# A feed-forward stage beside the attention: its last two experts take two PSUM banks in turn instead of three

## The chip, the cores and the metric

The kernel runs on one core of one Trainium2 chip. The time is device time of one execution in microseconds; the figure for a kernel is the median of its runs. TensorE (PE) does the matrix products, ScalarE (ACT) and VectorE (DVE) read their results out of PSUM, GpSimd (POOL) works on SBUF alone, and SyncE (SP) issues the DMAs.

## The reference

Three stages follow each other on 2304 tokens of width 512. All of it is in fp32.

- Attention over 4 batches, 8 heads, 576 positions of 64: scores, of each row only the 32 largest are kept, softmax over these, product with v.
- A first layer: `h = x @ w_in` (512 to 2048), `g = h * cos(h)`, `x2 = g @ w_out` (2048 to 512).
- A mixture of 8 experts: gate weights P come from `x2 @ w_gate` by eight rounds of row and column normalisation; each expert is `relu(x2 @ w1[e]) @ w2[e]` (512 to 1024 to 512), and the output is the sum over the experts of P[:, e] times its result, for all tokens.

## The kernel before

**Arithmetic.** An fp32 product is made of three matmuls of reduced precision: each operand is split into a high and a low part, and high by high, low by high and high by low are added up in one PSUM bank (`mm3`, lines 372 to 374). A weight block of 128x512 is loaded to a buffer `raw`; ACT copies its high part to `whi` (L345), POOL subtracts for the low part `wlo` (L347; in the layers after the attention DVE does that).

**Stages.** The first three tiles of 128 tokens (LEAD = 3) are taken through attention and the first layer early, then the rest of the attention runs batch by batch. It is DVE work above all: to find the 32nd largest score of a row takes four MAX8 and three MATCH_REPLACE8 over 576 columns per tile (L459, L464, L465), then one pass that masks and sums (L466). PE does little for it: the scores (L447, L448), the transposes (L475) and the product with v (L501, L503).

**Fill.** So that PE has work beside the attention, the experts of finished tokens are run beside it. `fill(e, t0, k, h_ring)` (line 762) does expert e for k tiles from t0: for each of 8 blocks f of the hidden width, 12 matmuls make `h` in a bank that it takes from `h_ring` (4 chunks of the model width, three matmuls each), `gates` reads it out twice (L758 on ACT: relu and high part `gh`; L759 on DVE: low part `gl`), and one block later 12 matmuls by w2 add to the four banks y0 to y3. After the eighth block y0 to y3 are copied to `st` (L788) and stored to `y_d`. Eight experts are filled beside batches 0 and 1 with tiles 0 to 2, a first layer of four tiles runs beside batch 1, and eight experts beside batches 2 and 3 with tiles 3 to 6. This last loop, the second block of fills, is the one that the change is in.

**Banks.** PSUM has eight: y0 to y3, `h`, `t` (transposes and the product with v), `s` (scores) and `g`. `two` is a cycle over `g` and `h`, `three` one over `g`, `s` and `h` (line 1004). Each call takes the next bank of the cycle. The scores of every attention tile go to `s`, and ACT reads them out (L457).

**Order.** Nothing is issued as it is written. Every operation is added to a plan with a cost, what it reads and writes and a priority by engine and kind of work (line 28: on PE attention 2 goes ahead of 3 for everything here called mlp, fills included; on DVE mlp 0 goes ahead of attention 2). An operation depends on the earlier ones *in program order* that wrote what it reads, and on those that read or wrote what it writes. `issue` (line 150) then plays the engines forward, takes the ready operation of the lowest priority number each time, and that makes each engine's fixed order. On the chip an engine goes through its order one by one and waits at each for its semaphores. In program order the attention of batches 2 and 3 stands wholly ahead of the eight fills.

**After.** `moe1` runs the first layer for the remaining tokens in three parts over the cycle `three` (lines 1027 to 1029), with a sixth weight buffer `ch`/`cl` (line 1024) in the pool `ph2`, which opens when the last user of the pools `att` and `ph1` is done: attention and the fills' input `x2fh` are among those. Its first five blocks by w_in and the sixth weight, of w_out, take the six buffers in turn. Then comes the mixture for the rest of the tokens, to the end.

```
    two, three = Cycle([ps_g, ps_h]), Cycle([ps_g, ps_s, ps_h])
    ...
    for b in range(2, B):
        attention(b)
    for e in range(NE):
        fill(e, LEAD, 4, two if e < 6 else three)
```

Of the kernel before, what the change touches and what calls it, by code (L numbers as in the profile page):

```python
# [217 lines left out]
def act_ns(n, psum=False, ap=False):  # L218
    return (51.0 if psum else 93.0) + n / 1.2 + (93.0 if ap else 0.0)
# [10 lines left out]
def fused_kernel(tc, kq, vv, w_in, w_out, w_gate, w1, w2, out, B=4):  # L230
# [14 lines left out]
    LEAD, FILL, MIXED = 3, 7, 8  # L245
# [16 lines left out]
    def put(eng, cost, emit, reads=(), writes=(), func=None, nbytes=0):  # L262
        return add(eng, cost, emit, reads, writes, PRIORITY[eng][CLASSES.index(work)], func, nbytes)

    def dma(dst, src, nbytes, reads=(), writes=(), slow=False):
        put("SP", 650.0 if slow else 475.0, lambda: nc.sync.dma_start(dst(), src()), reads, writes, nbytes=nbytes)
# [85 lines left out]
    def split_weight(src, dst=None):  # L352
        raw = raw_r()
        dma(lambda: raw.ap, lambda: src, 1 << 18, writes=[raw])
        hi, lo = dst or (whi_r(), wlo_r())
        split_cols((hi, lambda: hi.ap), (lo, lambda: lo.ap), (raw, lambda: raw.ap), eng=eng_w)
        return hi, lo
# [12 lines left out]
    def mm3(o, ob, ah, al, bh, bl, n, start, stop, bufs):  # L370
        def emit():
            T_.matmul(o(), ah(), bh(), start=start, stop=False)  # L372
            T_.matmul(o(), ah(), bl(), start=False, stop=False)  # L373
            T_.matmul(o(), al(), bh(), start=False, stop=stop)  # L374

        put("PE", 3 * mm_ns(n), emit, bufs, [ob])
# [378 lines left out]
    def gates(v, vb, n, g_r, psum):  # L755

        gh, gl = g_r()
        put("ACT", act_ns(n, psum=psum), lambda: A_.activation(gh.ap[:, :n], v(), AF.Relu), [vb], [gh])  # L758
        put("DVE", dve_ns(n), lambda: V.scalar_tensor_tensor(gl.ap[:, :n], v(), 0.0, gh.ap[:, :n].bitcast(F32), op0=ALU.max, op1=ALU.subtract), [vb, gh], [gl])  # L759
        return gh, gl  # L760

    def fill(e, t0, k, h_ring):

        n, pend = 128 * k, []

        def second(f, gh, gl):
            oh, ol = split_weight(w2[e, f])
            for t in range(k):
                c = slice(t * 128, t * 128 + 128)
                mm3(lambda t=t: ps_y[t].ap, ps_y[t], lambda c=c: gh.ap[:, c], lambda c=c: gl.ap[:, c], lambda: oh.ap, lambda: ol.ap,  # L770
                    512, f == 0, f == NF2 - 1, [oh, ol, gh, gl])

        for f in range(NF2):
            wh, wl = split_weight(w1[e, f])
            pb = h_ring()
            for c in range(4):
                s = slice(c * 128, c * 128 + 128)
                iv = (c * 512, c * 512 + 512)
                mm3(lambda pb=pb: pb.ap[:, :n], pb, lambda s=s, wh=wh: wh.ap[:, s], lambda s=s, wl=wl: wl.ap[:, s],
                    lambda c=c: x2fh.ap[:, c, :n], lambda c=c: x2fl.ap[:, c, :n], n, c == 0, c == 3, [wh, wl, (x2fh, *iv), (x2fl, *iv)])  # L780
            pend.append((f, *gates(lambda pb=pb: pb.ap[:, :n], pb, n, lambda: (gh_r(), gl_r()), True)))
            if len(pend) > 1:
                second(*pend.pop(0))
        second(*pend.pop(0))
        for t in range(k):
            st = st_r()
            i = e * FILL + t0 + t
            put("ACT", act_ns(512, psum=True), lambda t=t, st=st: A_.activation(st.ap, ps_y[t].ap, AF.Copy), [ps_y[t]], [st])  # L788
            dma(lambda t=t: y_d.ap[e, t0 + t], lambda st=st: st.ap, 1 << 18, [st], [(y_d, i, i + 1)])
# [214 lines left out]
    two, three = Cycle([ps_g, ps_h]), Cycle([ps_g, ps_s, ps_h])  # L1004
# [7 lines left out]
    for b in range(2, B):  # L1012
        attention(b)
    for e in range(NE):
        fill(e, LEAD, 4, two if e < 6 else three)


    eng_w = eng_r = eng_g = "DVE"
# [75 lines left out]
```

## Time and profile before

| | us |
|---|---|
| median of 3 runs | 2526.36 (2522.58 to 2527.22) |
| the profiled execution | 2523.42 |
| its span, first to last instruction | 2521.6 |
| PE busy | 2389.5 (95%) |
| DVE busy | 1981.5 (79%) |
| ACT busy | 1272.9 (50%) |
| POOL busy | 1265.6 (50%) |

The profile is of one execution. A view by windows gives each engine's busy time in a stretch and the clock that TensorE was granted there, 1.00 being 2.4 GHz and 0.50 1.2 GHz. In a timeline each line has the start in us, the duration, engine, line and operation, output <- inputs, and in brackets the idle time before it with what ended it. Matmuls overlap: one lasts some 0.39 us, and the next starts 0.23 us after it, so starts are compared, not durations.

### The profile page before, as it was taken

Reading aid. Unit: us, or ns where it says so; the run is one execution under the profiler, and the core shown is the slowest. Engines: PE = TensorE matmul, PEld = TensorE weight load, DVE = VectorE, ACT = ScalarE, POOL = GpSimd, SP = SyncE. Lnnn points to the kernel's source line nnn. Section 1 sums busy time; section 2 is a strip of 40 time slices with the busy share of each in tenths; the row PEclk is TensorE's granted clock in tenths of the full one; section 3 lists DMA queues with packets and bytes.
Section 4 is the critical chain, followed back from the end, with each engine's and each line's share of the span. In section 5 each row is a group of like instructions: output and inputs, shape, how many; then the busy total and the mean of one; then the engine's idle time right before and its main releaser. Section 6 shows DMA issues by size and latency. Waiting matters only on the chain.

```text
span 2521.6 us, 33547 instructions
## 1 busy us (share of the span) xinstructions
PE 2389.5 (95%) x11089; PEld 1919.8 (76%) x11089; DVE 1981.5 (79%) x3651; ACT 1272.9 (50%) x2438; POOL 1265.6 (50%) x1328
## 2 busy tenths in 40 slices
PE   6888999999889999997799999999999999999999
PEld 3444688888667877776588788788888888888887
DVE  8997599999989999999927778776666665666655
ACT  6785576666578656565346767422222222232221
POOL 6886587777676656565340113533333434444330
PEclk9779999999899999998799999999999999999999
DMA  8765654444322433332043333112222221111101
GB/s 265 228 211 185 201 155 150 137 139 131 99 91 78 120 116 117 109 117 77 26 132 114 106 108 115 48 55 79 71 72 84 84 72 34 34 34 46 38 21 46
DMA packets 159501, 261.37 MB, mean 104 GB/s; under 512 B 15008, under 2 KB 60656, under 8 KB 159328
## 3 DMA queue, kind: packets, MB, share of 16 engines
q1 hardware_dynamic: 159328, 259.24, 33.9%
q8 instruction: 87, 1.43, 0.2%
q14 instruction: 86, 0.70, 0.1%
HBM read 227.31 MB, written 31.87 MB: 103 GB/s over the span
## 4 chain that ended last, share of the span: by engine, by line
PE 56%; DVE 22%; POOL 4%; issue 3%; ACT 3%; DMA 1%; POOLq 0%; ACTq 0%; DVEq 0%
PE y L372 9%; PE y L373 9%; PE y L374 9%; DVE wk L464 6%; DVE m L465 5%; DVE ex L466 3%; PE g L374 2%; PE g L373 2%; PE g L372 2%; DVE atl L494 2%; DVE m L459 2%; POOL wlo L347 1%; PE y L383 1%; PE y L384 1%; PE y L387 1%
## 5 line engine op out<-in xcount | busy, mean ns | idle before, releaser
L347 POOL TENSOR_TENSOR wlo<-raw,whi 128x512 fp32r<-128x512 f32 x336 | 452.7, 1351 | 203.0 <-ACT whi L345 131.9
L465 DVE MAX8 m<-wk 128x8 f32<-128x576 f32 x432 | 318.0, 748 | 1.8
L953 DVE SCALAR_TENSOR_TENSOR acc<-y,P,acc 128x512 f32<-128x512 f32 x308 | 229.2, 748 | 103.4 <-PE y L374 103.0
L345 ACT ACTIVATE whi<-raw 128x512 fp32r<-128x512 f32 x416 | 258.9, 626 | 97.3 <-PE y L374 34.0
L464 DVE MATCH_REPLACE8 wk<-m,wk 128x576 f32<-128x576 f32 x288 | 213.6, 742 | 1.2
L475 PE MATMUL t<-ident,ex 128*128 128x128 f32 (+1 forms) x720 | 143.3, 301 | 55.8 <-DVE atl L494 20.6
L475 PEld LDWEIGHTS t<-ident,ex 128*128 128x128 f32 (+1 forms) x720 | 89.5, 145 | 122.3 <-DVE atl L494 32.4
L372 PE MATMUL y<-whi,gh 128*128 128x512 f32 x448 | 181.6, 405 | 0.0
L372 PE MATMUL y<-gh,xh 128*128 128x512 f32 x450 | 176.0, 391 | 1.0 <-DVE acc L949 1.0
L374 PE MATMUL y<-whi,gl 128*128 128x512 f32 x448 | 176.5, 394 | 0.0
L373 PE MATMUL y<-wlo,gh 128*128 128x512 f32 x448 | 175.9, 393 | 0.0
L373 PE MATMUL y<-gl,xh 128*128 128x512 f32 x450 | 175.5, 390 | 0.0
L374 PE MATMUL y<-gh,xl 128*128 128x512 f32 x450 | 175.4, 390 | 0.0
L457 ACT ACTIVATE sc<-s 128x288 f32<-128x288 f32 x288 | 117.0, 406 | 97.4 <-DVE ex L466 55.6
L466 DVE SCALAR_TENSOR_TENSOR ex<-sc,m,ex 128x576 f32<-128x576 f32 x144 | 149.7, 1039 | 3.6 <-ACT ex L461 1.8
L493 ACT ACTIVATE ath<-t 64x128 fp32r<-64x128 f32 (+3 forms) x272 | 104.5, 396 | 58.9 <-PE t L475 52.2
L470 POOL TENSOR_SCALAR ex<-ex,m 128x576 f32<-128x576 f32 x144 | 111.4, 774 | 38.1 <-DVE m L469 36.0
L461 ACT ACTIVATE ex<-sc,m 128x576 f32<-128x576 f32 x144 | 111.2, 772 | 32.1 <-POOL m L460 31.0
L459 DVE MAX8 m<-sc 128x8 f32<-128x576 f32 x144 | 106.9, 743 | 8.7 <-ACT sc L457 8.6
L464 DVE MATCH_REPLACE8 wk<-m,sc 128x576 f32<-128x576 f32 x144 | 106.7, 741 | 0.0
L468 POOL TENSOR_SCALAR m<-m 128x1 f32<-128x1 f32 x144 | 29.2, 202 | 146.5 <-DVE ex L466 141.3
L372 PEld LDWEIGHTS y<-gh,xh 128*128 128x128 f32 x450 | 84.5, 188 | 19.6 <-DVE acc L949 1.8
(384 smaller groups left out, 7150.5 us busy)
## 6 DMA issues: line engine op xcount, KB each, us to landing
raw<-in_w_dram SPq DMA_DIRECT2D x384, 256.0 KB, 2.6
kq<-in_kq_dram SPq DMA_DIRECT2D x32, 576.0 KB, 4.1
raw<-win_d SPq DMA_DIRECT2D x64, 256.0 KB, 3.0
raw<-wout_d SPq DMA_DIRECT2D x64, 256.0 KB, 2.7
y_d<-st SPq DMA_DIRECT2D x56, 256.0 KB, 3.0
raw<-y_d SPq DMA_DIRECT2D x56, 256.0 KB, 2.6
wp<-win_d SPq DMA_DIRECT2D x24, 512.0 KB, 5.0
wp<-wout_d SPq DMA_DIRECT2D x24, 512.0 KB, 4.4
```

The costliest lines, as they stand in the source:

```text
L345: put("ACT", act_ns(n), lambda: A_.activation(hv(), rv(), AF.Copy), [rb], [hb])
L347: put(e, c, lambda: f.tensor_tensor(lv(), rv(), hv().bitcast(F32), op=ALU.subtract), [rb, hb], [lb])
L372: T_.matmul(o(), ah(), bh(), start=start, stop=False)
L373: T_.matmul(o(), ah(), bl(), start=False, stop=False)
L374: T_.matmul(o(), al(), bh(), start=False, stop=stop)
L457: put("ACT", act_ns(288, psum=True), lambda c=c: A_.activation(sc.ap[:, c], o(), AF.Copy), [ps_s], [(sc, c.start, c.stop)])
L459: put("DVE", 669, lambda: V.max(mc(0, 8), sc.ap), [sc], [(m, 0, 8)])
L464: put("DVE", 669, lambda r=r, src=src: V.match_replace(wk.ap, mc(8 * r, 8), src.ap, LOWEST), [src, (m, 8 * r, 8 * r + 8)], [wk])
L465: put("DVE", 669, lambda r=r: V.max(mc(8 * r + 8, 8), wk.ap), [wk], [(m, 8 * r + 8, 8 * r + 16)])
L466: put("DVE", 729, lambda: V.scalar_tensor_tensor(ex.ap, sc.ap, mc(31), ex.ap, op0=ALU.is_ge, op1=ALU.mult, accum_out=mc(33)), [sc, ex, (m, ...
L475: T_.transpose(pt()[:p, c - c0, :], ex.ap[:, c * 128 : c * 128 + p], ident.ap)
L953: put("DVE", 663, lambda y=y, av=av, pcol=pcol: V.scalar_tensor_tensor(av(), y.ap, pcol(), av(), op0=ALU.mult, op1=ALU.add), [y, P, a], [a])
```

## The change

All eight fills of the second block take their `h` bank from `two`; experts 6 and 7 no longer take `s` in their turn. The two cycles keep a running position: `two` is called 16 times more, `three` 16 times less, so that the first-layer parts behind it begin at `g` where they began at `s`. No operation is added or left out.

```diff
     for b in range(2, B):
         attention(b)
     for e in range(NE):
-        fill(e, LEAD, 4, two if e < 6 else three)
+        fill(e, LEAD, 4, two)
```

## Rows read from the trace of the kernel before

**Rows 1.** The page's part 2: busy tenths in 40 slices of 63 us.

```profile
PE   6888999999889999997799999999999999999999
DVE  8997599999989999999927778776666665666655
```

**Rows 2.** Windows: length, busy us by engine (PE, PEld, DVE, ACT, POOL), clock, DMA.

```profile
820.00:1155.00 335.00, 329.76 (x1658) 267.10 (x1657) 329.54 (x716) 203.05 (x436) 203.67 (x259) 1.00 0.38 114
1155.00:1174.50 19.50, 19.46 (x105) 15.71 (x103) 19.23 (x43) 14.33 (x31) 12.37 (x16) 1.00 0.40 117
1610.00:2521.60 911.60, 905.26 (x4121) 762.68 (x4120) 589.37 (x877) 244.90 (x427) 339.94 (x294) 1.00 0.18 55
```

**Rows 3.** Timeline of PE around the dip, and one line of ACT.

```profile
1174.13 0.40 PE L374 MATMUL g<-x2fh,wlo 128*128 128x512 f32 x1
1175.27 0.30 PE L475 MATMUL t<-ident,ex 128*64 128x128 f32 x1 [0.75 <-DVE atl L494]
...
1232.24 0.41 ACT L457 ACTIVATE sc<-s 128x288 f32<-128x288 f32 x1 [0.92 <-PE s L448]
...
1232.70 0.79 PE L372 MATMUL s<-x2fh,whi 128*128 128x512 f32 x1
...
1321.94 0.39 PE L374 MATMUL y<-whi,gl 128*128 128x512 f32 x1
1322.17 0.39 PE L372 MATMUL s<-xh,whi 128*128 128x512 f32 x1
```

**Rows 4.** Windows between those seams, same columns.

```profile
1174.13:1232.70 58.57, 30.09 (x108) 20.74 (x106) 57.86 (x134) 23.07 (x51) 14.94 (x32) 0.60 0.07 18
1232.70:1271.50 38.80, 36.42 (x170) 28.91 (x170) 28.93 (x66) 15.16 (x32) 16.25 (x19) 0.94 0.21 59
1271.50:1322.17 50.67, 50.67 (x221) 41.34 (x220) 8.82 (x13) 22.10 (x38) 23.07 (x18) 1.00 0.47 139
```

**Rows 5.** Waits of PE, 1174.13 to 1232.7: total us, times, longest.

```profile
PE s L447 <- ACT sc L457: 10.5, 13, 2.6
PE t L475 <- DVE atl L494: 9.9, 7, 2.1
```

**Rows 6.** Timeline of the DMAs that SP issued there.

```profile
1208.06 31.16 SPq L266 DMA_DIRECT2D x_d<-x  x4
```

**Rows 7.** DVE by line, 1000 to 1100: busy us, mean ns, idle.

```profile
L465 DVE MAX8 m<-wk 128x8 f32<-128x576 f32 x38 | 28.0, 747 | 0.1
...
L466 DVE SCALAR_TENSOR_TENSOR ex<-sc,m,ex 128x576 f32<-128x576 f32 x13 | 14.9, 1144 | 0.1
...
L759 DVE SCALAR_TENSOR_TENSOR gl<-g,gh 128x512 fp32r<-128x512 f32 x7 | 4.7, 674 | 0.0
L759 DVE SCALAR_TENSOR_TENSOR gl<-h,gh 128x512 fp32r<-128x512 f32 x6 | 4.0, 672 | 0.0
```

**Rows 8.** The same by line, 1174.5 to 1232.7.

```profile
L465 DVE MAX8 m<-wk 128x8 f32<-128x576 f32 x25 | 18.3, 747 | 0.0
...
L466 DVE SCALAR_TENSOR_TENSOR ex<-sc,m,ex 128x576 f32<-128x576 f32 x9 | 7.5, 829 | 0.1
```

**Rows 9.** Window 1174.13 to 1271, line L759 (gl) alone: DVE busy, times.

```profile
1174.13:1271.00 96.87, 3.40 (x5) 0.74 0.13 34
```

**Rows 10.** Timeline of DVE: end of the attention, first use of cl.

```profile
1256.67 0.82 DVE L466 SCALAR_TENSOR_TENSOR ex<-sc,m,ex 128x576 f32<-128x576 f32 x1
...
1270.99 0.48 DVE L509 TENSOR_TENSOR x<-t,avt 64x320 f32<-64x320 f32 x1 [2.22 <-ACT avt L508]
...
1322.27 0.69 DVE L347 TENSOR_TENSOR cl<-raw,ch 128x512 fp32r<-128x512 f32 x1 [1.21 <-ACT ch L345]
```

**Rows 11.** Timeline of PE and DVE: two h banks read out.

```profile
1283.25 0.39 PE L374 MATMUL g<-x2fh,wlo 128*128 128x512 f32 x1
...
1284.31 0.69 DVE L759 SCALAR_TENSOR_TENSOR gl<-g,gh 128x512 fp32r<-128x512 f32 x1 [2.12 <-ACT gh L758]
1289.85 0.69 DVE L759 SCALAR_TENSOR_TENSOR gl<-s,gh 128x512 fp32r<-128x512 f32 x1 [4.84 <-ACT gh L758]
```

## The prediction

> **What bounds the kernel now.** I read the page's slices first. Two engines take turns: DVE stands at nine tenths or more in nearly every slice from the 6th to the 20th and then drops, and PE stands at nine from the 21st on [rows 1]. At the turn, in the 19th and 20th slices, PE shows 7: the last dip of PE, and it lies just where the changed fills are. So windows come next. From 820 to 1155 us attention and fill together hold both engines: PE 329.76 and DVE 329.54 of 335 us; from 1610 to the end PE is busy 905.26 of 911.6 us [rows 2]. What PE still has to do when the attention thins out is therefore added to the end of the kernel one to one, and an idle us of PE ahead of that is a us of the total.
>
> The timeline shows the dip's edges [rows 3]. At 1174.13 starts the last matmul of a group of a fill (x2fh into bank g), and then PE does attention alone. At 1232.24 ACT reads the last scores out of bank s, 0.41 us long, and at 1232.70 PE starts the next fill group: into bank s. By the program this is expert 6, block 1: blocks 0, 2 and 3 of that expert take g, h and g, block 1 takes s, and a writer of s waits for every reader of s ahead of it in program order, so for the scores of the whole attention of batches 2 and 3. Blocks 2 and 3 could go past it, but block 1's weight stays in one of five buffers, so the second product of block 2 gets none, and the fill stands. In those 58.57 us PE is busy 30.09 at a mean granted clock of 0.60, DVE 57.86 [rows 4]. PE waits there for the attention's own steps, scores read out (10.5 us in 13 waits) and transposes read out (9.9 in 7) [rows 5]: DVE sets the pace, and PE has nothing to put between.
>
> **The change part by part.** Nothing is added or removed; a dependence goes. With g and h alone, block 1 of expert 6 waits only for its own cycle's reader, as the blocks of experts 0 to 5 do, and these ran up to here at PE 19.46 of 19.50 us [rows 2].
>
> What moves: of the two experts' 32 groups of 12 matmuls (8 blocks by w1 and 8 by w2 each) four are done by 1174.13 (blocks 0, 2, 3 by w1, block 0 by w2). The other 28, 336 matmuls, stand between 1232.70 and 1322.17, where the next layer begins [rows 3]. With the bank free they spread from 1174.13 on between the attention's pieces.
>
> PE's sum is the work from 1174.13 to 1322.17 (148.04 us) laid end to end at full clock [rows 4]:
> - First stretch, attention alone, 30.09 us busy. At the granted 0.60 this would be 18.1 us at 1.00; if all of it ran at 1.2 GHz, half, 15.0. The mean of 0.60 takes in the idle parts, and lone bursts also show drains that back-to-back work hides, so I stay near the lower end: 15.5. Ends kept: 15.0 to 18.1.
> - Second, 38.80 us: 36.42 busy at 0.94, so 34.2 at full clock.
> - Third, 50.67 us, all busy at 1.00.
> Together 100.4 (99.9 to 103.0). In the mixed stretch PE idles 335 - 329.76 = 5.24 us, 1.6% [rows 2]; the same share here is 1.6. So the next layer begins 102.0 us after 1174.13, at 1276.1 and not 1322.17: 46.0 us gained, 43.5 to 48.1 with those ends and that idle share; with no idle, up to 48.1 + 1.6 = 49.7.
>
> What comes along, and its cover: each block also brings two weights (POOL L347, ACT L345, one DMA each), a read-out on ACT (L758) and one on DVE (L759). POOL is busy 14.94 and ACT 23.07 of the 58.57 us, the DMA engines 0.07 [rows 4]; in the mixed stretch they carry the same load per us of fill at 203.67 and 203.05 of 335 [rows 2], so these cost nothing. SP's queue holds four stores of attention results from 1208 to 1239 and no load [rows 6]; the loads of weights move past them, at a DMA share that was 0.38 in the mixed stretch. If the cover failed, PE would wait for a weight once per group; rows of the mixed stretch, where it doesn't, are the nearest.
>
> DVE is the one without slack, so the attention ends later. Nine more gl than before fall ahead of its end (14 blocks had theirs to come, 5 of these ran by 1271 [rows 9]), at 0.67 us each [rows 7]: 6.0 us. And L466 took 829 ns with the fill away, 1144 ns beside it [rows 7, 8]; 13 tiles pass it from here on (9 in the stretch, 4 later), so 13 x 0.315 = 4.1 us. The attention's last step, at 1270.99 [rows 10], moves to about 1281. Upper bound by tiles: 13 in 100 us beside the fill [rows 7], 9 in 58.2 without [rows 8], 1.2 us more each, so 15.9 us: 1287. Lower bound: the gl alone, less than 6.0 since some fall behind the end; not below nothing, since no DVE work goes.
>
> MAX8, which has one input, took 747 ns in both windows, and L466, which reads sc and ex from SBUF, is the one that stretched [rows 7, 8]. The Trainium skill (GPSIMD Engine Reference, 1. Specifications) says that GpSimd's SBUF interfaces are shared with VectorE and contended by DVE instructions with two SBUF inputs; by that rule moving POOL's splits back beside the attention costs DVE at L466 alone, and the trace agrees. It speaks against the change, and the 4.1 us above are its price here.
>
> What is late next: the new end of the attention, 1281 to 1287, lies behind the new start of the next layer, 1276. That layer's first five groups by w_in use old buffers and tokens of batches 1 and 2, stored long before; its sixth weight goes to ch, which opens only with the attention's end. Before, cl was written at 1322.27, 51 us after the attention [rows 10]. A group of 12 lasts half of the 5.54 us from gl to gl [rows 11], 2.77, so five cover 13.9 us, to 1290. That holds, with 3 to 9 us to spare. Behind 1322.17 all moves up unchanged; the other phase of the cycle of three changes which bank is first, with all three free by then. I cost that at nothing, 2 us either way for the seam at the gate stage.
>
> The sum is against the profiled execution, 2523.4: 2477.4. The median shown is 2526.4, 2.9 above it, which gives 2480.4. I forecast 2479.
>
> **The rivals.**
> *A, the attention's end becomes the bound.* Place: the weight in ch. If the attention moved not by 10 to 16 but by 30 us (2.3 us for each of 13 tiles, twice the bound above), ch would open at 1301 and PE lose 11 us; add the fill's groups waiting in PE's order behind attention steps with the idle share at 6% and not 1.6% (4 to 5 us more), and 30 of the 46 us are left: 2496. For it: DVE has 0.7 us of slack in 58.57. Against: 1155 to 1174.5 ran the same mix without a gap [rows 2]. Chance 0.17, for any gain of 20 to 42.
>
> *B, slower: two banks are too few.* Place: the bank of each h group. The next group into a bank must wait until gl has left it, and with g and h that is every second block where with three it was every third. The turn now: last matmul issued at 1283.25, gl done at 1285.00, 1.75 us, plus the group's 2.77 is 4.5 us; the bank is wanted again after 2 x 5.54 = 11.1 [rows 11]. It begins to cost where a turn exceeds 11.1, and loses more than the 46 gained where each of the 13 h groups left stalls over 3.5 us, at turns above 18: DVE would have to reach gl 13 us late. At 5 us per group it is 65 lost, 2526 + 19 = 2545. Against it: six experts ran on these two banks with DVE full. Chance 0.03. The Trainium skill (Perfetto Trace Analysis, Matmul Optimizations) asks for all eight banks to be used; that rule would have this change lose, by this mechanism.
>
> *C, the bank was not the hold.* Something else of expert 6 (y banks, weights, loads) holds it, and the fill stays put: 2526. For it: loads stop too [rows 6]. Against: block 0 ran through both products before the stall, and the first group after it goes into s 0.05 us after the last scores left it [rows 3]. Chance 0.04.
>
> **How the numbers follow.** The forecast (42 to 50 gained) 0.73, A 0.17, B 0.03, C 0.04, more than 50 gained 0.03. The forecast's own range, from either base, is 2474 to 2484. With A's nearer half the range is 2472 to 2495. Within 0.2% (5 us, about what can be told from no change) is C; B is slower; the rest is faster: 0.93, 0.04, 0.03.
>
> **What would show it.** Right: the trace after has matmuls by x2fh without a gap across 1174 to 1232 at clock 1.00; PE busy about 57 of those 58 us; no bank s among the fill's outputs; the attention's last step near 1281; the next layer's first matmul (xh) near 1276, into g; behind it the same 1200 us. Wrong: PE gaps that end with gl (B) or with ch (A), an attention end beyond 1290, or an unchanged gap with another releaser (C).

## The result, and the profile after

The changed kernel took 2481.27 us (median of 4 runs, 2480.17 to 2482.34) against 2525.93 of the kernel before (4 runs): a ratio of 0.9825, 95% interval 0.9808 to 0.9842, 44.7 us less. The forecast was 2479 in a range of 2472 to 2495. Spans of the two profiled executions: 2478.7 and 2521.6, 42.9 less.

The page's slices of the changed kernel: the 7s of PE in the 19th and 20th slices [rows 1] are gone.

```profile
PE   6878999999889999999999999999999999999999
DVE  8997599999998999999986787776666666666655
```

The windows, columns as in [rows 2]. From 820 to 1155 us nothing differs beyond 0.4 us of any engine. In the stretch where PE was busy 30.09 of 58.57 us at a clock of 0.60 [rows 4] it is now busy 58.36 at 1.00, and DVE is as full as it was (57.87 against 57.86).

```profile
820.00:1155.00 335.00, 329.72 (x1658) 267.22 (x1657) 329.37 (x716) 203.07 (x435) 204.02 (x258) 1.00 0.38 114
1155.00:1174.13 19.13, 19.10 (x105) 15.68 (x104) 18.94 (x40) 13.77 (x29) 12.14 (x15) 1.00 0.40 117
1174.13:1232.70 58.57, 58.36 (x296) 47.50 (x295) 57.87 (x132) 36.02 (x75) 33.31 (x43) 1.00 0.35 99
1232.70:1271.50 38.80, 38.33 (x185) 30.84 (x184) 36.35 (x76) 20.91 (x41) 20.36 (x25) 1.00 0.41 123
```

The timeline of PE at the two edges of [rows 3]. After the same time stamp the fill goes straight on, with transposes and scores between its groups; the next layer (xh) begins at 1269.20 where it began at 1322.17, in bank g.

```profile
1174.11 0.39 PE L372 MATMUL y<-whi,gh 128*128 128x512 f32 x1
...
1175.08 0.30 PE L475 MATMUL t<-ident,ex 128*64 128x128 f32 x1
1175.13 0.38 PE L447 MATMUL s<-kh,qs 128*128 128x288 f32 x1
...
1176.18 0.39 PE L372 MATMUL g<-x2fh,whi 128*128 128x512 f32 x1
...
1268.98 0.39 PE L374 MATMUL y<-whi,gl 128*128 128x512 f32 x1
1269.20 0.39 PE L372 MATMUL g<-xh,whi 128*128 128x512 f32 x1
```

Of PE's waits from 1174 to 1290 (total us, times, longest) one is left; before, it waited for the scores alone 10.5 us [rows 5].

```profile
PE t L475 <- POOL ex L470: 0.4, 1, 0.4
```

The end of the attention and the first use of the sixth weight buffer, timelines of DVE and PE, answering to [rows 10].

```profile
1267.02 0.82 DVE L466 SCALAR_TENSOR_TENSOR ex<-sc,m,ex 128x576 f32<-128x576 f32 x1
...
1291.94 0.48 DVE L509 TENSOR_TENSOR x<-t,avt 64x320 f32<-64x320 f32 x1
...
1296.61 0.69 DVE L347 TENSOR_TENSOR cl<-raw,ch 128x512 fp32r<-128x512 f32 x1
...
1297.27 0.39 PE L383 MATMUL y<-gh,ch 128*128 128x512 f32 x1
```

The new start of the layer is 52.97 us earlier, the end only 42.9. Some 4 us of the difference, most of it attention work of PE that now lies behind the start (18 matmuls of the product with v, five transposes; 3.1 us from start to start), is gone by the last w_out group but two of the layer: its last matmuls (L387) start at 1568.82 before and at 1520.10 after, 48.7 us apart. The rest is lost just behind that place, where the layer meets the gate stage and the mixture (the seam, from here on): from there to the end the changed kernel takes 958.6 us and the kernel before 952.8, 5.8 less, for the same work. All of it is lost ahead of the last 4000 matmuls, for which the two kernels need 884.3 and 884.2 us. The first experiments are on that, the later ones on the main gain.

### The profile page after: what moved, and what is told of

It is laid out like the page before. It is cut to its first block, busy times and chain, and to the rows that moved or that the text cites. A ratio compares the mean times of both kernels' runs of the same rounds, so it can differ in the third digit from the quotient of the medians.

```text
span 2478.7 us, 33516 instructions
## 1 busy us (share of the span) xinstructions
PE 2364.7 (95%) x11089; PEld 1905.7 (77%) x11089; DVE 1986.9 (80%) x3651; ACT 1271.7 (51%) x2438; POOL 1266.6 (51%) x1328
## 4 chain that ended last, share of the span: by engine, by line
PE 57%; DVE 28%; POOL 6%; issue 4%; ACT 3%; DMA 1%; SPq 0%; POOLq 0%; ACTq 0%; DVEq 0%
PE y L372 9%; PE y L373 9%; PE y L374 9%; DVE wk L464 7%; DVE m L465 6%; DVE ex L466 4%; PE g L374 2%; PE g L373 2%; PE g L372 2%; DVE m L459 2%; POOL wlo L347 2%; DVE atl L494 1%; PE y L383 1%; PE y L387 1%; PE y L384 1%
## 5 line engine op out<-in xcount | busy, mean ns | idle before, releaser
L347 POOL TENSOR_TENSOR wlo<-raw,whi 128x512 fp32r<-128x512 f32 x336 | 451.7, 1349 | 195.1 <-ACT whi L345 116.3
L475 PE MATMUL t<-ident,ex 128*128 128x128 f32 (+1 forms) x720 | 136.6, 290 | 39.7 <-POOL ex L470 10.9
L466 DVE SCALAR_TENSOR_TENSOR ex<-sc,m,ex 128x576 f32<-128x576 f32 x144 | 152.8, 1061 | 3.6 <-ACT ex L461 1.8
L372 PE MATMUL y<-gh,gh 128*128 128x512 f32 x254 | 99.4, 391 | 0.0
```

The lines of the kernel that those rows point to most:

```text
L347: put(e, c, lambda: f.tensor_tensor(lv(), rv(), hv().bitcast(F32), op=ALU.subtract), [rb, hb], [lb])
L466: put("DVE", 729, lambda: V.scalar_tensor_tensor(ex.ap, sc.ap, mc(31), ex.ap, op0=ALU.is_ge, op1=ALU.mult, accum_out=mc(33)), [sc, ex, (m, ...
L475: T_.transpose(pt()[:p, c - c0, :], ex.ap[:, c * 128 : c * 128 + p], ident.ap)
```

## The experiments

Each kernel was timed against the kernel before: the first four on one chip, beside 15 runs of before (median 2523.99), the last four on another, beside 13 (2522.99).

**The changed kernel again**, as it is, for the next three to stand beside.

> The changed kernel itself, timed beside the next three on one chip. Both theories: the same as measured, 2481 us (2479 to 2484), 0.9825 of before.

Measured: 2481.27 us (2480.01 to 2481.90), ratio 0.9830 [0.9817, 0.9844].

**The phase of the three banks.** The change leaves the cycle `three` at another position, and the forecast priced that at nothing, give or take 2 us. Here it is put back by hand:

```diff
+    three.i += 1
     moe1(Part(n0 + 512, three, keep_raw(acc, 0)), 2)
```

> The changed kernel, with the cycle of three advanced by one ahead of the first-layer parts, so that these begin at bank s as in the kernel before. Theory (the 6 us given back at the seam to the mixture come from the banks' phase: the logits of the last part take h, and the mixed product that wants h can't fill PE's wait of 3.56 us): PE's waits from the last w_out group but two to the end fall from 8.6 to about 6 us, the clock there stays at 0.97, and the time is 5 to 6 us lower, 2475 us. Rival (the 6 us come from the attention's later end or from the planner's other order): the same as the changed kernel, 2481 us.

Measured: 2476.60 us (2471.64 to 2477.53), ratio 0.9808 [0.9795, 0.9822]: 4.7 us under the changed kernel, and no run of the one in the range of the other. The rival falls: the fills run without the gap as in the changed kernel, the attention's last step begins as late (1293.68, there 1291.94), the seam is reached 1.7 us later than there (1521.82), and from it to the end this kernel takes 952.6 us, as before the change. I had expected the clock in the window at the seam to stay at 0.97; it was 1.00 (windows below).

**The third position**, with `three.i += 2`:

> The changed kernel, with the cycle of three advanced by two, so that the parts begin at h and the last logits take s. Theory of the phase: the bank h is free for the mixed product as in the kernel before, but s, which the first mixed product takes, is late; between the two, 2475 to 2481 us, 2478 if half. Rival (no phase): 2481 us.

Measured: 2475.54 us (2473.55 to 2478.59), ratio 0.9808 [0.9795, 0.9821], 5.7 us under the changed kernel. I had expected a value between the two; it is as good as the position before, with 952.4 us from the seam to the end: s taken by the logits costs nothing that these runs show.

**The old fills with the new phase**: the kernel before with `three.i += 2` at the same line.

> The kernel before, its fills unchanged, with the cycle of three advanced by two, so that the first-layer parts begin at g as in the changed kernel. Theory of the phase: the seam loses what the changed kernel loses there, 5 to 6 us, so 2531 us, and the dip beside the attention stays. Rival (no phase): 2526 us.

Measured: 2528.35 us (2527.10 to 2531.82, 11 runs), ratio 1.0021 [1.0012, 1.0030]: 4.4 us lost, with the dip beside the attention still there. From the seam to the end it takes 956.9 us. So the phase alone does it, in either kernel.

The timelines of PE show how. A line has start, duration, operation, and in brackets the idle time ahead of it. First the kernel before, then the changed kernel, then the one with the phase put back:

```profile
1569.61 0.42 PE L803 MATMUL t<-ident,st 16*128 16x16 f32 x4
1571.54 0.74 PE L885 MATMUL h<-th,whi 128*128 128x512 f32 x1 [1.51 <-ACT whi L345]
...
1574.79 0.46 PE L383 MATMUL y<-gh,whi 128*128 128x384 f32 x1
...
1580.73 0.33 PE L602 MATMUL g<-xrh,wg 128*16 128x384 f32 x1
```

```profile
1520.89 0.42 PE L803 MATMUL t<-ident,st 16*128 16x16 f32 x4
1524.87 0.44 PE L383 MATMUL y<-gh,whi 128*128 128x384 f32 x1 [3.56 <-ACT gh L345]
...
1531.31 0.35 PE L602 MATMUL h<-xrh,wg 128*16 128x384 f32 x1
```

```profile
1522.61 0.42 PE L803 MATMUL t<-ident,st 16*128 16x16 f32 x4
1524.24 0.50 PE L885 MATMUL h<-th,whi 128*128 128x512 f32 x1 [1.22 <-ACT whi L345]
...
1533.44 0.33 PE L602 MATMUL g<-xrh,wg 128*16 128x384 f32 x1
```

While the layer's last gates come out of ACT, PE has one thing ready: a product of the mixture (L885), which by the program always takes bank h. Before the change the logits that stand ahead of it in program order (L602) went to g, so it could go first. In the changed kernel they go to h, the product must wait for their readers, and PE stands 3.56 us. The windows of 51.9 us from the seam on, one of each kernel (before, changed, phase put back, old fills with the new phase):

```profile
1568.82:1620.70 51.88, 48.23 (x226) 38.12 (x226) 32.30 (x59) 27.36 (x49) 33.80 (x30) 0.97 0.19 56
```

```profile
1520.10:1572.00 51.90, 45.95 (x210) 36.53 (x210) 31.07 (x56) 27.90 (x49) 31.77 (x27) 0.93 0.18 55
```

```profile
1521.80:1573.70 51.90, 47.29 (x228) 37.40 (x227) 33.00 (x60) 28.18 (x50) 33.79 (x29) 1.00 0.20 60
```

```profile
1568.40:1620.30 51.90, 45.64 (x210) 36.33 (x210) 31.03 (x56) 27.68 (x49) 31.74 (x27) 0.93 0.20 55
```

The first busy time, with its count, is PE's: 226 and 228 matmuls where the logits don't take h, 210 and 210 where they do. Sixteen matmuls at some 0.23 us are 3.7 us, and with h taken the granted clock of the window is lower too, 0.93. The other 2 us of the 5.8 fall in the stretch right behind this window, up to the last 4000 matmuls: 22.40 us in the changed kernel and 16.74 before, for those sixteen matmuls more. What takes them was not tried.

**Expert 6 alone back on three banks.** Here and in the next two runs a line `three.i += ...` ahead of the first-layer parts, not shown, makes them begin at s, as before the change.

```diff
-        fill(e, LEAD, 4, two)
+        fill(e, LEAD, 4, three if e == 6 else two)
```

> Of the changed kernel, expert 6 alone goes back to three banks (its blocks 1, 4 and 7 to s), expert 7 keeps two; the first-layer parts begin at s as before the change. Theory (one writer of s in program order behind the attention holds the whole fill, since the experts share the y banks and the five weight buffers): no gain is left, PE stands from 1174 to 1232 as before, 2526 us (2520 to 2530). Rival (each expert gains for itself): half the gain, about 2503 us.

Measured: 2523.35 us (2521.49 to 2524.81, 10 runs), ratio 1.0000 [0.9991, 1.0010]. All of the gain is gone, and the gap is where it was, from 1173.66 to 1232.47 on PE's timeline:

```profile
1173.66 0.40 PE L374 MATMUL g<-x2fh,wlo 128*128 128x512 f32 x1
1174.81 0.30 PE L475 MATMUL t<-ident,ex 128*64 128x128 f32 x1 [0.75 <-DVE atl L494]
...
1232.47 0.79 PE L372 MATMUL s<-x2fh,whi 128*128 128x512 f32 x1
```

Expert 7's two banks are worth nothing while expert 6 stands ahead of it in the y banks and the weight buffers.

**Expert 7 alone back on three banks** (`three if e == 7 else two`).

> Expert 7 alone goes back to three banks, expert 6 takes two; the parts begin at s. Theory: the fill now stands at block 1 of expert 7, 16 groups of 12 matmuls later (12 of expert 6, 4 of expert 7, 44 us of PE beside some 12 us of attention), so from about 1231 to the last scores read out, near 1240: a dip of some 9 us and not 58; 2484 us (2478 to 2490). Rival (each expert gains for itself): about 2503 us.

Measured: 2485.37 us (2484.01 to 2487.33), ratio 0.9850 [0.9835, 0.9864]; 1.4 us from the expected 2484. The window on the gap, which was expected from 1231 to 1240 (PE busy 4.74 of 8.11 us at 0.70):

```profile
1233.81:1241.92 8.11, 4.74 (x21) 3.52 (x19) 7.80 (x19) 3.98 (x9) 2.47 (x5) 0.70 0.24 73
```

**Three banks one expert earlier**, in the kernel before (`two if e < 5 else three`).

> The kernel before, with three banks for experts 5, 6 and 7 (s one expert earlier); the parts begin at s. Theory (the first writer of s sets where the fill stops): PE's dip begins 16 groups earlier, near 1118, its end some 8 us earlier than 1232 since less fill work is on DVE, and 16 groups of 2.77 us more come behind the attention: 36 to 44 us slower than before, 2562 to 2570 us. Rival (the count of experts on three banks): 23 us slower, 2549 us.

Measured: 2564.55 us (2561.42 to 2565.12), ratio 1.0159 [1.0142, 1.0176]: 41.6 us slower than before. The gap grows to 113.78 us, from 1114.74 to 1228.52, its end 4 us earlier than before (8 expected): DVE makes one gl in it, where the kernel before makes nine between these times.

```profile
1114.74:1228.52 113.78, 62.95 (x218) 45.40 (x217) 112.56 (x259) 45.65 (x103) 30.35 (x63) 0.55 0.05 15
```

These three settle the main step: the first block in program order whose bank the attention also writes sets where the fill stops, and what stands behind it waits with it. A count of experts on three banks would have given 2503 twice and 2549.

**One bank.** All eight experts of the block take g alone:

```diff
+    one = Cycle([ps_g])
-        fill(e, LEAD, 4, two)
+        fill(e, LEAD, 4, one)
+    three.i += 1
     moe1(Part(n0 + 512, three, keep_raw(acc, 0)), 2)
```

> All eight experts of the second block take the one bank g for their h groups; the parts begin at s. Theory by the bank's turn (group 2.77 us, read out 1.75 to 3 us behind it, wanted again one block later, some 7.1 us beside the attention and 5.54 without): the product by w2 covers the turn, at most 5 us lost against the two banks with the same phase, 2477 to 2482 us. Rival (h groups must rotate through banks, or PE stands while ACT and DVE read them out): at least 1.75 us for each of 64 blocks, 112 us, 2590 us.

Measured: 2494.91 us (2494.07 to 2499.57), ratio 0.9891 [0.9876, 0.9905]: 18 us over the two banks with the same phase (19 when each is taken against its own runs of before), still 28 us under the kernel before. Neither theory's figure held: 18 us is over my 5 and far under the rival's 112, some 0.3 us per block and not 1.75. PE's waits from 756 to 1300, one bank first, two banks with the same phase below:

```profile
PE t L475 <- DVE atl L494: 7.6, 10, 1.8
PE g L372 <- DVE gl L759: 6.6, 6, 1.7
PE s L447 <- ACT sc L457: 4.8, 10, 1.5
```

```profile
PE t L475 <- DVE atl L494: 2.9, 5, 0.8
...
PE s L447 <- ACT sc L457: 1.7, 3, 1.0
```

Only 6.6 us is PE waiting for the bank itself, in six blocks; at two of the attention's own steps it waits 4.7 and 3.1 us more. I read this as the planner's order putting other work into most read-outs, and PE being early at the attention's steps where none is ready; no run tests that reading.

## Why the prediction was right, step by step

- *What holds the fill: block 1 of expert 6, in bank s.* Right, shown by the fifth to seventh experiments. Rival C, that something else held it, fell with the result, where the gap is gone.
- *PE's work from 1174.13 laid end to end, next layer at 1276.1.* It began at 1269.20, with some 4 us of the attention's PE work left behind, so the same work was done near 1273, some 3 us better. The idle share is one part: 95.07 us to the layer's start with 94.39 busy, 0.7 us idle and not 1.6. The rest lies in the 100.4 of work at full clock, and there in the attention's matmuls: from start to start they take 18.6 us in the changed kernel, 15.5 ahead of the layer's start and 3.1 behind it. The forecast had 15.5 for the first stretch alone, and in the second some 8 more by its own figures (34.2 less 115 matmuls of the fill, which are its 336 less the 221 of the third stretch, at 0.23).
- *ACT, POOL and the DMAs cover what moves along.* Right: PE has no wait for a weight from 1174 to 1290.
- *The attention's end, by DVE's terms, 1281 and at most 1287.* Wrong: it came at 1292.4, beyond the 1290 that the prediction names as a sign against it. The last L466 began at 1267.02, 10.35 us later than in [rows 10], as the two terms' 10.1 say, but by other parts. There were 14 gl ahead of it where before there were three, since two of the five of [rows 9] came behind the old last L466: eleven more at 0.68 us, 7.5. L466 was busy 11.07 us against 10.01 in the two windows from 1174.13 to its last start, 1.1 more; the first of its 12 tiles lies mostly ahead of that window in the changed kernel, and over all 12 the times add up to 12.3 against 9.9, 2.3 more and not 4.1. Three splits of the next layer's weights (L347), at some 0.6 us each, made up the rest. Behind it the tail took 25.4 us, before 14.8: the next layer's work on ACT and DVE goes ahead of the attention's last steps. The last product with v ended at 1281.18; ACT read it out 5.3 us later, behind work that includes an ACT_TABLE_LOAD of 1.28 us for the next layer's cosine, and DVE came to the last step 5.0 us after that. Before, both went on at once. That I had not counted.

```profile
1280.87 0.31 PE L501 MATMUL t<-ath,vs 128*128 128x320 f32 x1
1281.98 1.28 ACT L592 ACT_TABLE_LOAD   x1
...
1286.50 0.43 ACT L508 ACTIVATE avt<-t 64x320 f32<-64x320 f32 x1
```

- *Cover for the late end: five groups of the next layer, to 1290.* The late end cost nothing, but the margin was not the one that I named. PE ran nine groups of that layer, up to 1297.27, ahead of its first product from ch, since later blocks use old buffers too. cl was written behind the attention's end, at 1296.61, and PE did not wait for it; so the late end that rival A feared came in part, and its price did not.
- *Rival B, two banks are too few.* It fell: no wait for a bank is left. The Trainium skill (Perfetto Trace Analysis, Matmul Optimizations) asks that all eight banks be used. All eight are still in use here, but leaving one of them to its other user gained 44.7 us, and even one bank for the h groups was faster than three of which one is shared with work far ahead in program order. Rotation as such does pay: the second bank is worth 18 us.
- *Behind 1322.17 all moves up unchanged, the phase of the cycle at nothing, 2 us either way.* This is the term that was mis-sized: 4.7 us by the second experiment, 4.4 by the fourth, 5.8 in the two traces. All three banks are free when the parts begin, as I said, but I looked at the cycle's start and not at where it ends 51 calls later.

So the mechanism was right, but that 46.0 forecast and 44.7 measured lie so close is luck, two errors that nearly cancel: 3 us too little for the stretch, some 5 too much behind it.

## What to carry to other kernels

Where an order is planned from program order, a shared buffer ties its users together across everything written between them: a block that takes its turn in a bank of work far ahead waits for the last of that work, and all that shares its other buffers waits too. Look for the first such block, not for how many there are; and when a rotating buffer's users change in number, follow the cycle to where it ends, since its phase decides which later work may fill a wait. The phase put back gives a version faster than both, 2476.60 us.

## What had not been expected of the hardware

L466, an operation of DVE with two inputs in SBUF, took 829 ns with POOL's weight splits all but away [rows 8], 1144 beside them earlier in the kernel [rows 7], and 905 in the seven tiles of the changed kernel from 1174.5 to 1232.7, where POOL was busy 33.31 of 58.57 us. A mean over so few tiles says little: the eleven tiles from 1180.80 to 1258.80 lasted 797 to 1448 ns, 972 in the mean.

The traces show what sorts them: which of the two operations begins first. Two pairs of lines from the changed kernel:

```profile
1203.81 1.29 POOL L347 TENSOR_TENSOR wlo<-raw,whi 128x512 fp32r<-128x512 f32 x1 [1.72 <-issue]
1204.57 1.15 DVE L466 SCALAR_TENSOR_TENSOR ex<-sc,m,ex 128x576 f32<-128x576 f32 x1
...
1180.80 0.81 DVE L466 SCALAR_TENSOR_TENSOR ex<-sc,m,ex 128x576 f32<-128x576 f32 x1
1181.13 1.62 POOL L347 TENSOR_TENSOR wlo<-raw,whi 128x512 fp32r<-128x512 f32 x1 [2.57 <-ACT whi L345]
```

In the first, the split was running when L466 began, and L466 ended 0.62 us after the split did. In the changed kernel from 820 to 1270 us there are 23 tiles that began with at least 0.25 us of a split (L347 on POOL) still to run, and all of them ended 0.61 or 0.62 us behind its end; they lasted 0.91 to 2.03 us. One more, begun 0.01 us ahead of a split, did the same (1.92 us). In the second pair L466 began first, took its usual time, and the split lasted 1.62 us where 1.3 is usual. So the forecast's term hangs on where the splits happen to fall: between 1000 and 1100 us before the change, seven of 13 tiles began inside a split of POOL, with 0.8 us of it left in the mean; of the eleven tiles named above it was six, with 0.5 us left. No run moved the splits on purpose.
